# Reads of a compressive memory: full-array matmuls in the slot of the weighted sums, or matmuls on halves of the array's rows one slot later

## The chip, the cores and the metric

The kernel runs on one core of a Trainium2 chip. Five engines work side by side, each through its own instructions in order: TensorE (PE, matmuls and transposes, with weight loads shown apart as PEld), VectorE (DVE), ScalarE (ACT), GpSimd (POOL) and SyncE (SP, which here only issues DMAs). Matmuls write to PSUM, which the kernel uses as eight banks of 128 x 512 fp32; DVE and ACT read it. The metric is the device time of one execution in microseconds (us), the median of several.

## The reference

Four layers follow each other on x of 2048 rows by 512: A, B, A, B. A is linear attention with a learned feature map, B is attention in four segments of 512 rows with a memory that runs over the segments. The change is in B:

```python
phi = lambda t: jnp.where(t > 0, t + 1.0, jnp.exp(t))
for s in range(N):                      # N = 4 segments, H = 32 heads, Dh = 16
    qs, ks, vs = q[:, :, s], k[:, :, s], v[:, :, s]
    logits = jnp.einsum("bhqd,bhkd->bhqk", qs, ks) * scale + mask
    p = _softmax(logits, axis=-1)
    a_dot = jnp.einsum("bhqk,bhkd->bhqd", p, vs)
    pq = phi(qs)
    num = jnp.einsum("bhld,bhde->bhle", pq, M)
    den = jnp.einsum("bhld,bhd->bhl", pq, z)[..., None] + 1e-6
    a_mem = num / den
    o = g * a_mem + (1.0 - g) * a_dot
    outs.append(o)
    pk = phi(ks)
    M = M + jnp.einsum("bhld,bhle->bhde", pk, vs)
    z = z + jnp.einsum("bhld->bhd", pk)
```

A "read" is num, den and a_mem: the features of the queries against the memory M and its sums z. The memory is empty in the first segment, so segments 1 to 3 read it.

## The kernel before, in words

**Tiling.** Heads are handled in four chunks of eight (c = 0 to 3). The query features of one segment and chunk lie with 128 partitions (8 heads x 16) by 512 rows. A memory chunk `kn` is 128 partitions by 8 x 17 columns (16 values and one sum for each head), block diagonal: partitions 0 to 63 belong to heads 0 to 3 and 64 to 127 to heads 4 to 7, and the rest is zero. A read's output `ot` has 128 rows by four row blocks by 8 heads x 16.

**Order.** The program is fully unrolled, and the order is written out by hand. The helper `held` puts all matmuls and transposes in one fixed order on PE; the class `Ordered` does the same for DVE, ACT, POOL and SP: each engine executes in the order in which the Python code emits. In the profile all matmuls bear L178, transposes L182, and all other instructions L156, so groups are told by tile names and shapes.

**Slots.** The loop of B (`steps`) runs over slots k. Each unit of work m (four heads of one segment; 8 units a segment, 32 in all) takes R = 5 slots, named m.0 to m.4 within a segment. Each slot emits, in this order:

1. `attend`: one tile of logits into `lg` (PE), its exp by ACT into P, the masked blocks by POOL;
2. `maxima`: one step of row maxima for a later unit: products (PE) into `mx` and `my`, or in slots m.2 and m.4 (`SPARE`) into two banks of `g`, and their reduction by DVE ("CUSTOM_DVE_ANT_0 ... mask");
3. jobs that were put off to this slot, such as the low part `ta` of a projection (ACT copies the high part, DVE subtracts), and the DMAs that stack parts;
4. in m.0 alone `weighted`: P times v (PE, "g<-P,v"), evicted by ACT into U;
5. the words of the table's cell for this slot, left to right.

The tables FIRST, GAPS (segments 1 and 2), LAST and FINAL (segment 3 of the first and the second loop) hold the cells. The words that matter here: `a0` to `a3` one step of the read of chunk 0 to 3 (a `+` means the next segment); `max` transposes finished maxima ("g<-ident,mxs"), `fin` transposes U ("g<-ident,U"), weighs it on DVE and adds it to `ot` on POOL; `t`, `m` the two steps of a memory write; `ln` a step of a norm, which transposes x and makes its high and low parts; `Q`, `V`, `O` with `/6` six steps of a pair of projections, values or outputs; `v` work of the next layer. A pair is two accumulations at once on the two halves of the array's rows (`mm3_pair`); it takes its two banks of `g` at its first step in m.1 and gives them back after m.4.

**PSUM.** Tag `g` has four banks (G = 4), `lg` two, `mx` and `my` one each. A tile of `g` that finds all four in use waits until readers have finished with one.

**Weighing.** `weigh` takes a PSUM tile: DVE adds 1e-6 to the sums (reads only), takes reciprocals ("r<-r") and multiplies ("ot<-g,r"); for `fin` the product goes to `wt`, which POOL adds.

**The reads before.** `reads` has two steps, one for each half of the row blocks: one bank of `g`, two matmuls of 128 rows by 136 columns in fp32 ("g<-mem,tb"; each shows as two passes in the profile), one `weigh`. They stand in slots m.0, most often both steps ahead of `max` and `fin`.

Of the kernel before, what the change touches and what calls it, by code (L numbers as in the profile page):

```python
# [18 lines left out]
P = 128  # L19
# [3 lines left out]
VW = DH + 1  # L23
# [8 lines left out]
G = 4  # L32
# [27 lines left out]
4.0 max fin        | 4.1 Q0+/6 load    | 4.2 Q0+/6         | 4.3 Q0+/6 | 4.4 Q0+/6  # L60
5.0 t2 fin m2 max  | 5.1 V+/6          | 5.2 V+/6 n        | 5.3 V+/6 n | 5.4 V+/6
6.0 t3 fin m3 max  | 6.1 Q1+/6         | 6.2 Q1+/6 n       | 6.3 Q1+/6 n | 6.4 Q1+/6
7.0 a0+ a0+ max fin | 7.1 V+/6         | 7.2 V+/6 n        | 7.3 V+/6 n | 7.4 V+/6
"""
GAPS = """
0.0 a1 a1 max fin  | 0.1 Q2/6 n        | 0.2 Q2/6 n        | 0.3 Q2/6 n | 0.4 Q2/6
1.0 t0 turn fin m0 max | 1.1 Q3/6      | 1.2 Q3/6 n        | 1.3 Q3/6 | 1.4 Q3/6
2.0 turn t1 fin ln m1 max | 2.1 O/6    | 2.2 O/6           | 2.3 O/6 | 2.4 O/6
3.0 turn turn fin ln max | 3.1 O/6     | 3.2 O/6           | 3.3 O/6 | 3.4 O/6
4.0 ln ln a2 fin a2 max | 4.1 Q0+/6 load | 4.2 Q0+/6       | 4.3 Q0+/6 | 4.4 Q0+/6  # L70
5.0 t2 a3 fin m2 max | 5.1 V+/6 begin  | 5.2 V+/6 n N      | 5.3 V+/6 n N | 5.4 V+/6
6.0 a3 t3 fin m3 max | 6.1 Q1+/6       | 6.2 Q1+/6 n N     | 6.3 Q1+/6 n N | 6.4 Q1+/6
7.0 a0+ a0+ max fin | 7.1 V+/6         | 7.2 V+/6 n N      | 7.3 V+/6 n N | 7.4 V+/6
"""
LAST = """
0.0 a1 a1 max fin  | 0.1 Q2/6 n        | 0.2 Q2/6 n        | 0.3 Q2/6 n | 0.4 Q2/6
1.0 turn max fin   | 1.1 Q3/6          | 1.2 Q3/6 n        | 1.3 Q3/6 | 1.4 Q3/6
2.0 turn ln fin max | 2.1 O/6          | 2.2 O/6           | 2.3 O/6 | 2.4 O/6
3.0 turn turn fin ln max | 3.1 O/6     | 3.2 O/6           | 3.3 O/6 | 3.4 O/6
4.0 ln ln a2 fin a2 max | 4.1 v/2      | 4.2 v/2           | 4.3 v/2 | 4.4 v/2  # L80
5.0 a3 a3 max fin  | 5.1 v/1           | 5.2 v/1           | 5.3 v/1 | 5.4 v/1
6.0 max fin        | 6.1 v/1           | 6.2 v/1           | 6.3 v/1 | 6.4 v/1 pre
7.0 pt pt fin max  | 7.1 P/4           | 7.2 P/5           | 7.3 P/5 v/2 | 7.4 P/4 v/2
"""
FINAL = """
0.0 a1 a1 max fin  | 0.1 Q2/6          | 0.2 Q2/6          | 0.3 Q2/6 | 0.4 Q2/6
1.0 turn turn max fin | 1.1 Q3/6       | 1.2 Q3/6          | 1.3 Q3/6 | 1.4 Q3/6
2.0 max fin        | 2.1 O/6           | 2.2 O/6           | 2.3 O/6 | 2.4 O/6
3.0 a2 a2 max fin  | 3.1 O/6           | 3.2 O/6           | 3.3 O/6 | 3.4 O/6
4.0 turn turn fin max | 4.1 O/6        | 4.2 O/6           | 4.3 O/6 | 4.4 O/6  # L90
5.0 a3 a3 max fin  | 5.1 O/6           | 5.2 O/6           | 5.3 O/6 | 5.4 O/6
6.0 max fin pre    | 6.1 pt pt         | 6.2 P/6           | 6.3 P/6 | 6.4 P/6
7.0 pt pt max fin  | 7.1 P/4           | 7.2 P/5           | 7.3 P/5 | 7.4 P/4
"""
# [6 lines left out]
def interleave_kernel(ctx, tc, x_in, a_wqkv, a_wphi, a_wo, b_wq, b_wk, b_wv, b_wo, b_beta,  # L101
# [15 lines left out]
    def nm(s):  # L117
        uid[0] += 1
        return f"{s}_{uid[0]}"

    def T2(tag, bufs, dt=F32, shape=(P, 512)):
        return sp.tile(list(shape), dt, tag=tag, bufs=bufs, name=nm(tag))

    def PS(tag, bufs, shape=(P, 512)):
        return ps.tile(list(shape), F32, tag=tag, bufs=bufs, name=nm(tag))
# [40 lines left out]
    def held(i):  # L166

        if last[0] is not None:
            behind(i, last[0])
        last[0] = i  # L170
        return i
# [3 lines left out]
    def mm(*a, **k):  # L175
        n = a[0].free_size()
        work[0] += n / 2.26 if k["rhs"].dtype == F32R else (n * 2 / 2.4 + 25 if "tile_position" in k else 2 * max(112, n * 2 / 2.4))
        return held(nc.tensor.matmul(*a, **k))  # L178
# [339 lines left out]
    def weigh(out, p, eps, add, eng=pool):  # L518

        n, G = out.shape[1], out.shape[2]  # L520
        r = T2("r", 4, shape=(P, n, G))
        den = p[:, :, :, DH]
        if eps:
            dve.tensor_scalar(r, den, eps, None, op0=ADD)
            den = r
        dve.reciprocal(r, den)
        rb = r.unsqueeze(3).broadcast_to([P, n, G, DH])
        if not add:
            dve.tensor_tensor(out=out, in0=p[:, :, :, 0:DH], in1=rb, op=MUL)
            return  # L530
        t = T2("wt", 1, shape=(P, n, G, DH))
        dve.tensor_tensor(out=t, in0=p[:, :, :, 0:DH], in1=rb, op=MUL)
        eng.tensor_tensor(out=out, in0=out, in1=t, op=ADD)
# [441 lines left out]
    class LayerB:  # L975
# [96 lines left out]
        def reads(self, s, c):  # L1072

            kn = self.mem[:, c, 1]
            ph = self.st[s, c]["phi", 0]
            ot = self.sums(s, c).rearrange("p q (h d) -> p q h d", d=DH)
            for a in range(2):
                pn = PS("g", G)
                for q in range(2):
                    mm(pn[:, q * 8 * VW : (q + 1) * 8 * VW],  # L1080
                       lhsT=ph[:, (2 * a + q) * P : (2 * a + q + 1) * P], rhs=kn,
                       start=True, stop=True)
                weigh(ot[:, 2 * a : 2 * a + 2], pn[:, 0 : 16 * VW].rearrange("p (q h e) -> p q h e", q=2, h=8),
                      1e-6, False)
                yield

        def writes(self, s, c):

# [369 lines left out]
    for i in range(2):  # L1458
# [3 lines left out]
        a2 = la[i].pass2()  # L1462
# [40 lines left out]
```

## Time and profile before

| | |
|---|---|
| median of 3 runs | 1444.89 us (1442.71 to 1445.47) |
| the profiled execution | 1442.99 us |
| its span, first to last instruction | 1441.3 us |
| TensorE clock granted, mean | 0.997 |
| exps of the loops: 320 of 128 x 1024 on ACT | 329.3 us busy |
| reads on PE: 192 passes of 128 x 136 | 30.1 us busy |

How to read the lines: a group or a timeline row names the line, engine and operation, the tiles as out<-in, the shape (a matmul's shape is rows*columns of the array and then the moving operand), and xN for the number of instructions that were merged. In a timeline the first two columns are start and length in us; "[0.57 <-DVE mxs L156]" is idle time of the engine just before, and what ended it. A matmul's length includes its way through the pipeline, so the cost of one in a row of many is the distance of starts. A stretch lists, after its bounds and length, each engine's busy time in us with the number of instructions, then the granted clock, the DMA share and GB/s.

### The profile page before, as it was taken

What the parts mean: (1) busy time and instruction counts of PE and PEld (TensorE: products, weight loads), DVE (VectorE), ACT (ScalarE), POOL (GpSimd) and SP (SyncE); (2) the same over time, 40 slices, a digit from 0 to 9 for tenths busy, and PEclk for the clock granted to TensorE, in tenths of its full rate; (3) what the DMA queues carried; (4) which work ended last, traced back from release to release, by engine and by line L of the source; (5) the groups of instructions that cost most, each with busy time, mean ns of one, the idle gap of its engine ahead of it and who ended that gap; (6) DMA issues with size and microseconds to landing.
All of it is one profiled execution on the core that took longest, in us unless ns stands there. A gap on an engine that the chain in (4) does not pass through costs nothing.

```text
span 1441.3 us, 33697 instructions
## 1 busy us (share of the span) xinstructions
PE 1372.0 (95%) x12544; PEld 1049.0 (73%) x12544; DVE 1057.3 (73%) x3258; ACT 808.9 (56%) x1198; POOL 691.5 (48%) x1028
## 2 busy tenths in 40 slices
PE   7999989999999999999999999999999999999997
PEld 6887877776676776777568887887666767777764
DVE  4666778667787887888646767867768878878882
ACT  5545345436576577576634434453656756756653
POOL 1568665315447457335314446542335555654441
PEclk9999999999999999999999999999999999999998
DMA  5387356545444444445430103754453453443431
GB/s 193 115 317 270 127 159 192 161 118 154 119 126 141 117 132 137 118 130 166 141 125 22 60 30 129 249 171 120 125 178 97 131 157 97 130 130 97 112 91 59
DMA packets 108787, 196.06 MB, mean 136 GB/s; under 512 B 14416, under 2 KB 27856, under 8 KB 107856
## 3 DMA queue, kind: packets, MB, share of 16 engines
q1 hardware_dynamic: 107472, 193.38, 44.8%
q8 instruction: 100, 1.64, 0.5%
q10 hardware_dynamic: 1152, 0.52, 0.1%
q14 instruction: 63, 0.52, 0.1%
HBM read 101.05 MB, written 39.85 MB: 98 GB/s over the span
## 4 chain that ended last, share of the span: by engine, by line
PE 69%; DVE 12%; ACT 7%; POOL 5%; issue 3%; DMA 2%; SPq 1%; ACTq 0%; DVEq 0%; POOLq 0%
PE g L178 52%; PE lg L178 6%; PE g L182 5%; PE mx L178 3%; ACT P L156 3%; DVE es L156 2%; POOL tb L156 2%; POOL P L156 2%; PE lg L182 1%; PE my L178 1%; DVE g L156 1%; ACT U L156 1%; DMA wqk<-wqk 1%; DVE my L156 1%; DVE mx L156 1%
## 5 line engine op out<-in xcount | busy, mean ns | idle before, releaser
L156 ACT ACTIVATE P<-lg 128x1024 f32<-128x1024 f32 x320 | 329.3, 1029 | 176.9 <-PE lg L178 95.7
L156 POOL TENSOR_SCALAR_AFFINE_SELECT P<-P 128x256 f32<-128x256 f32 (+1 forms) x448 | 192.5, 444 | 327.3 <-ACT P L156 327.0
L156 DVE CUSTOM_DVE_ANT_0 mx<-mx,mask 128x128 f32<-128x128 f32 (+3 forms) x332 | 165.0, 497 | 42.6 <-PE my L178 37.8
L178 PE MATMUL g<-hh,wqk 64*128 64x512 f32 (+1 forms) x960 | 188.1, 392 | 3.5 <-DMA wqk<-wqk 2.0
L156 DVE CUSTOM_DVE_ANT_0 g<-g,mask 128x512 f32<-128x512 f32 x360 | 175.9, 543 | 15.2 <-PE g L178 14.4
L178 PE MATMUL g<-w,oh 64*128 64x512 f32 (+2 forms) x816 | 172.2, 385 | 6.8 <-SPq L156 5.0
L156 DVE CUSTOM_DVE_ANT_0 my<-my,mask 128x128 f32<-128x128 f32 (+3 forms) x332 | 172.0, 518 | 0.0
L178 PE MATMUL lg<-e,e 64*128 64x256 f32 (+2 forms) x1024 | 154.5, 353 | 14.5 <-ACT P L156 14.3
L178 PE MATMUL g<-P,v 128*32 128x512 f32 (+3 forms) x2048 | 151.1, 435 | 4.3 <-DVE mxs L156 4.0
L178 PE MATMUL g<-w,hh 64*128 64x512 f32 (+2 forms) x800 | 145.3, 357 | 0.6 <-DVE ol L156 0.6
L156 DVE DVE_READ_ACCUMULATOR2_ANT mxs<- 128x1 f32 x1024 | 143.2, 140 | 0.0
L178 PEld LDWEIGHTS lg<-e,e 64*128 64x128 f32 x1024 | 92.6, 185 | 64.3 <-ACT P L156 40.7
L178 PEld LDWEIGHTS g<-P,v 128*32 128x32 f32 x2048 | 59.7, 109 | 89.0 <-issue 63.8
L156 POOL TENSOR_SCALAR tb<-tb 128x512 f32<-128x512 f32 x72 | 110.9, 1552 | 25.4 <-ACT tb L156 22.1
L178 PEld LDWEIGHTS g<-hh,wqk 64*128 64x128 f32 (+1 forms) x960 | 108.2, 185 | 20.0 <-ACT hh L156 1.8
L178 PEld LDWEIGHTS g<-w,oh 64*128 64x128 f32 (+1 forms) x816 | 98.2, 188 | 28.9 <-SPq L156 9.6
L178 PE MATMUL g<-hl,wqk 64*128 64x512 f32 (+1 forms) x480 | 108.9, 390 | 0.5 <-DVE hl L156 0.5
L178 PE MATMUL g<-w,ol 64*128 64x512 f32 (+2 forms) x408 | 106.8, 379 | 1.0 <-DVE ol L156 1.0
L156 ACT COPY tb<-g 128x512 f32<-128x512 f32 (+1 forms) x148 | 80.9, 576 | 45.5 <-PE g L178 43.6
L178 PEld LDWEIGHTS g<-w,hh 64*128 64x128 f32 (+1 forms) x800 | 91.9, 187 | 13.3 <-DVE ol L156 1.0
L178 PE MATMUL g<-w,hl 64*128 64x512 f32 (+2 forms) x400 | 93.7, 355 | 0.0
L178 PE MATMUL mx<-e,e 63*128 63x256 f32 (+2 forms) x332 | 89.4, 331 | 0.3 <-DVE mxs L156 0.2
(148 smaller groups left out, 2917.3 us busy)
## 6 DMA issues: line engine op xcount, KB each, us to landing
e<-ta SPq DMA_DIRECT2D x384, 128.0 KB
wqk<-wqk SPq DMA_DIRECT2D x64, 512.0 KB
x<-x SPq DMA_DIRECT2D x48, 256.0 KB
ot<-in SPq DMA_DIRECT2D x28, 256.0 KB
pq<-tb SPq DMA_DIRECT2D x24, 256.0 KB
tb<-pq SPq DMA_DIRECT2D x24, 256.0 KB
x<-xr SPq DMA_DIRECT2D x22, 256.0 KB
xr<-x SPq DMA_DIRECT2D x20, 256.0 KB
```

Source lines behind the costliest of these rows:

```text
L156: i = f(*a, **k)
L178: return held(nc.tensor.matmul(*a, **k))
L182: return held(nc.tensor.transpose(*a))
```

## The change

The two steps of `reads` become one. It takes two banks of `g`, one for heads 0 to 3 and one for heads 4 to 7 of the chunk. For each of the four row blocks it issues two matmuls, on array rows 0 to 63 and 64 to 127, with 68 columns of `kn` each: the diagonal blocks alone. Then both banks are weighed. In the tables the word moves from m.0 to m.1, ahead of the pair in that cell; the two halves of a3, which stood in 5.0 and 6.0 in GAPS, come together in 5.1.

```diff
-7.0 a0+ a0+ max fin | 7.1 V+/6         | 7.2 V+/6 n        | 7.3 V+/6 n | 7.4 V+/6
+7.0 max fin        | 7.1 a0+ V+/6         | 7.2 V+/6 n        | 7.3 V+/6 n | 7.4 V+/6
...
 GAPS = """
-0.0 a1 a1 max fin  | 0.1 Q2/6 n        | 0.2 Q2/6 n        | 0.3 Q2/6 n | 0.4 Q2/6
+0.0 max fin        | 0.1 a1 Q2/6 n        | 0.2 Q2/6 n        | 0.3 Q2/6 n | 0.4 Q2/6
-4.0 ln ln a2 fin a2 max | 4.1 Q0+/6 load | 4.2 Q0+/6       | 4.3 Q0+/6 | 4.4 Q0+/6
-5.0 t2 a3 fin m2 max | 5.1 V+/6 begin  | 5.2 V+/6 n N      | 5.3 V+/6 n N | 5.4 V+/6
-6.0 a3 t3 fin m3 max | 6.1 Q1+/6       | 6.2 Q1+/6 n N     | 6.3 Q1+/6 n N | 6.4 Q1+/6
-7.0 a0+ a0+ max fin | 7.1 V+/6         | 7.2 V+/6 n N      | 7.3 V+/6 n N | 7.4 V+/6
+4.0 ln ln fin max       | 4.1 a2 Q0+/6 load | 4.2 Q0+/6       | 4.3 Q0+/6 | 4.4 Q0+/6
+5.0 t2 fin m2 max    | 5.1 a3 V+/6 begin  | 5.2 V+/6 n N      | 5.3 V+/6 n N | 5.4 V+/6
+6.0 t3 fin m3 max | 6.1 Q1+/6       | 6.2 Q1+/6 n N     | 6.3 Q1+/6 n N | 6.4 Q1+/6
+7.0 max fin         | 7.1 a0+ V+/6         | 7.2 V+/6 n N      | 7.3 V+/6 n N | 7.4 V+/6
...
 LAST = """
-0.0 a1 a1 max fin  | 0.1 Q2/6 n        | 0.2 Q2/6 n        | 0.3 Q2/6 n | 0.4 Q2/6
+0.0 max fin        | 0.1 a1 Q2/6 n        | 0.2 Q2/6 n        | 0.3 Q2/6 n | 0.4 Q2/6
-4.0 ln ln a2 fin a2 max | 4.1 v/2      | 4.2 v/2           | 4.3 v/2 | 4.4 v/2
-5.0 a3 a3 max fin  | 5.1 v/1           | 5.2 v/1           | 5.3 v/1 | 5.4 v/1
+4.0 ln ln fin max       | 4.1 a2 v/2      | 4.2 v/2           | 4.3 v/2 | 4.4 v/2
+5.0 max fin        | 5.1 a3 v/1           | 5.2 v/1           | 5.3 v/1 | 5.4 v/1
...
 FINAL = """
-0.0 a1 a1 max fin  | 0.1 Q2/6          | 0.2 Q2/6          | 0.3 Q2/6 | 0.4 Q2/6
+0.0 max fin        | 0.1 a1 Q2/6          | 0.2 Q2/6          | 0.3 Q2/6 | 0.4 Q2/6
-3.0 a2 a2 max fin  | 3.1 O/6           | 3.2 O/6           | 3.3 O/6 | 3.4 O/6
+3.0 max fin        | 3.1 a2 O/6           | 3.2 O/6           | 3.3 O/6 | 3.4 O/6
-5.0 a3 a3 max fin  | 5.1 O/6           | 5.2 O/6           | 5.3 O/6 | 5.4 O/6
+5.0 max fin        | 5.1 a3 O/6           | 5.2 O/6           | 5.3 O/6 | 5.4 O/6
...
-            for a in range(2):
-                pn = PS("g", G)
-                for q in range(2):
-                    mm(pn[:, q * 8 * VW : (q + 1) * 8 * VW],
-                       lhsT=ph[:, (2 * a + q) * P : (2 * a + q + 1) * P], rhs=kn,
-                       start=True, stop=True)
-                weigh(ot[:, 2 * a : 2 * a + 2], pn[:, 0 : 16 * VW].rearrange("p (q h e) -> p q h e", q=2, h=8),
-                      1e-6, False)
-                yield
+            pns = [PS("g", G)[:, 0 : 16 * VW] for _ in range(2)]
+            for q in range(4):
+                for a, pn in enumerate(pns):
+                    mm(pn[:, q * 4 * VW : (q + 1) * 4 * VW], lhsT=ph[64 * a : 64 * a + 64, q * P : (q + 1) * P],
+                       rhs=kn[64 * a : 64 * a + 64, 4 * a * VW : (4 * a + 4) * VW], start=True, stop=True,
+                       tile_position=(64 * a, 0))
+            for a, pn in enumerate(pns):
+                weigh(ot[:, :, 4 * a : 4 * a + 4], pn.rearrange("p (q h e) -> p q h e", q=4, h=4), 1e-6, False)
+            yield

```

## The prediction

> **What bounds the kernel now.** I read the page's busy shares first, then the by-engine line of the chain of waits, and then the stretch of the first attention loop.
>
> ```profile
> PE 1372.0 (95%) x12544; PEld 1049.0 (73%) x12544; DVE 1057.3 (73%) x3258; ACT 808.9 (56%) x1198; POOL 691.5 (48%) x1028
> ...
> PE 69%; DVE 12%; ACT 7%; POOL 5%; issue 3%; DMA 2%; SPq 1%; ACTq 0%; DVEq 0%; POOLq 0%
> ...
> 310.00:740.00 430.00, 412.19 (x4065) 300.38 (x4062) 325.97 (x1220) 277.45 (x399) 202.71 (x349) 1.00 0.47 134
> ```
>
> PE sets the end; in the loop it is busy 412 of 430 us. DVE is third in busy time (326 us of 430), but it matters here because PE hands it PSUM banks. The clock was granted in full, so no clock effect enters. Next, the tile view of the memory state gives the reads, and the timeline shows one of them, a1 in slot 0.0, and the two slots behind it (columns: start, length, engine, line, operation).
>
> ```profile
> L178 PE MATMUL g<-mem,tb x192: 279/279/384, 399.2 to 1393.6; 128*128 128x136 f32 x192
> ...
> 519.79 1.19 PE L178 MATMUL g<-mem,tb 128*128 128x136 f32 x8
> 519.92 0.69 ACT L156 ACTIVATE U<-g,share 128x512 f32<-128x512 f32 x1 [0.79 <-PE g L178]
> 520.56 0.17 DVE L156 TENSOR_SCALAR r<-g 128x16 f32<-128x16 f32 x1 [0.98 <-PE g L178]
> 520.82 0.27 PE L182 MATMUL g<-ident,mxs 128*16 128x128 f32 x1
> 520.93 0.60 PE L182 MATMUL g<-ident,U 128*128 128x128 f32 x4
> 521.05 0.42 DVE L156 TENSOR_TENSOR ot<-g,r 128x256 f32<-128x256 f32 x1
> 521.39 0.16 DVE L156 TENSOR_SCALAR r<-g 128x16 f32<-128x16 f32 x1
> 521.46 0.50 PE L178 MATMUL lg<-e,e 64*128 64x512 f32 x2
> 521.79 0.28 PE L178 MATMUL mx<-e,e 63*128 63x256 f32 x1
> 522.22 0.25 DVE L156 RECIPROCAL r<-g 128x16 f32<-128x16 f32 x1
> 522.50 0.42 DVE L156 TENSOR_TENSOR wt<-g,r 128x256 f32<-128x256 f32 x1
> 522.84 0.29 DVE L156 CUSTOM_DVE_ANT_0 mx<-mx,mask 128x128 f32<-128x128 f32 x1
> 523.49 0.46 PE L178 MATMUL lg<-e,e 64*128 64x256 f32 x4
> 523.78 0.39 PE L178 MATMUL g<-e,e 63*128 63x512 f32 x2
> 524.33 0.73 DVE L156 CUSTOM_DVE_ANT_0 g<-g,mask 128x512 f32<-128x512 f32 x1
> ```
>
> There are 192 read passes: 24 reads of four matmuls, each in two passes. Eight of them take 520.82 - 519.79 = 1.03 us with some 0.10 us for the first weights, so 0.93 us, or 0.116 us each. PE then transposes the maxima and U, and slot 0.1 begins with lg at 521.46. Nothing on PE waits. On DVE one weighing takes 0.83 us to the next (520.56 to 521.39) and 0.91 us to its own end (521.05 + 0.42), finish's weighing 0.62 (522.22 to 522.84), and the four maxima of slot 0.1 take 1.49 (522.84 to 524.33). The maxima of slot 0.2 start on PE at 523.78, which is 2.32 us behind the lg of 0.1.
>
> **The reads themselves: no time saved.** After, each read is 8 matmuls of 64 rows by 68 columns, 16 passes, in 8 pairs if the two halves run together. The trace has no fp32 row halves, so I bound a pair by its nearest rows: column halves with 68 columns below, row halves with the same 128 weight columns above.
>
> ```profile
> L178 PE MATMUL g<-KN,P 128*64 128x68 f32 x1024 | 38.2, 226 | 6.6 <-ACT P L156 6.6
> ...
> 201.85 1.17 PE L178 MATMUL g<-KN,P 128*64 128x68 f32 x32 [0.72 <-ACT P L156]
> ...
> 401.55 0.40 PE L178 MATMUL g<-w,hh 64*128 64x256 f32 x4
> 401.79 0.28 PE L178 MATMUL g<-w,hl 64*128 64x256 f32 x2
> ```
>
> The first: 16 pairs in 1.17 us less the last one's 0.23 of its own, 0.059 us each. The second: two pairs from 401.55 to 401.79, 0.12 us each. The shorter one loads 64 weight columns, the other 128 as the reads do, so I take 0.118: a read costs 8 x 0.118 = 0.94 us instead of 0.93. Bounds: 0.47 us, and 16 x 0.116 = 1.86 us if the halves do not overlap at all. The first read pass bears on this: it lasts 384 ns instead of 279, 105 ns longer for weights that nothing hides. The weighing's new view, four blocks of four heads, costs nothing: finish's product has that view already, and both products take 0.42 us (521.05, 522.50).
>
> The Trainium skill (TensorE: Matmul & The Clock Gate, section LDWEIGHTS) says that a weight load's time follows its columns and not its rows, about 107 ns for 128; the trace's 105 ns agrees. By it the halved rows do not make the loads shorter, and a read would cost 8 x 0.107 = 0.86 us, near my value.
>
> **The place: what the reads covered in x.0.** They stood between the weighted sums and the transposes, while ACT evicted U. Slots that have no read show what happens without them.
>
> ```profile
> 704.52 0.69 ACT L156 ACTIVATE U<-g,share 128x512 f32<-128x512 f32 x1 [1.47 <-PE g L178]
> 705.26 0.66 PE L182 MATMUL g<-ident,U 128*128 128x128 f32 x4 [0.60 <-ACT U L156]
> 705.95 0.26 DVE L156 RECIPROCAL r<-g 128x16 f32<-128x16 f32 x1 [1.74 <-PE g L182]
> ```
>
> U's transposes start 0.05 us after U's end (705.21) and wait 0.60 us; DVE starts 0.03 us after their end. So with the a1 read gone they start at 519.92 + 0.69 + 0.05 = 520.66 instead of 520.93: slot 0.0 gets 0.27 us shorter and not 0.93. The lg of 0.1 starts 0.53 us after that, at 521.19.
>
> **The two banks: a new wait in x.2.** Tag g has four banks. In x.1 the read now takes two and the pair of projections or outputs behind it takes the other two and keeps them to x.4. In x.2 the maxima ask for two g banks: only the read's can be free, and these come free when DVE has weighed both. DVE works in program order, so ahead of that stand finish's weighing, the four maxima of x.1 and, in some slots, the subtraction that makes a low part. For a1: U transposed at 520.66 + 0.60 = 521.26, DVE starts 521.29, finish 0.62 to 521.91, maxima 1.49 to 523.40 (their scores come at 521.52 + 0.28), weighings 0.83 + 0.91 to 525.14, bank seen by PE 0.05 later, 525.19. Before it was 523.78: **+1.41 us**. PE by itself would be there at 521.19 + 2.03 + 0.94 + 0.29 = 524.45, so 0.74 of this is waiting. Queued behind the waiting maxima on PE are that slot's six pairs, the next lg, and with it ACT's next exp. The halves' price hardly enters: a shorter read only lengthens the wait, and the 1.86 bound ends 0.5 us after DVE is free here.
>
> The same sum for the other reads, each with the rows it needs:
>
> ```profile
> 507.63 0.69 ACT L156 ACTIVATE U<-g,share 128x512 f32<-128x512 f32 x1 [0.86 <-PE g L178]
> 511.50 0.39 PE L178 MATMUL g<-e,e 63*128 63x512 f32 x2
> 512.11 0.69 DVE L156 TENSOR_TENSOR ta<-tb,ta 128x512 fp32r<-128x512 f32 x1
> 512.72 0.69 DVE L156 CUSTOM_DVE_ANT_0 g<-g,mask 128x512 f32<-128x512 f32 x1
> ...
> 576.57 0.16 DVE L156 TENSOR_SCALAR r<-g 128x16 f32<-128x16 f32 x1
> 579.42 0.40 PE L178 MATMUL g<-e,e 63*128 63x512 f32 x2
> ...
> 591.14 0.30 DVE L156 CUSTOM_DVE_ANT_0 mx<-mx,mask 128x128 f32<-128x128 f32 x1 [0.45 <-PE my L178]
> 592.80 0.40 PE L178 MATMUL g<-e,e 63*128 63x512 f32 x2
> ...
> 1392.86 0.69 ACT L156 ACTIVATE U<-g,share 128x512 f32<-128x512 f32 x1 [1.47 <-PE g L178]
> 1396.47 0.40 PE L178 MATMUL g<-e,e 63*128 63x512 f32 x2
> ...
> 399.37 0.69 ACT L156 ACTIVATE U<-g,share 128x512 f32<-128x512 f32 x1 [0.87 <-PE g L178]
> 402.60 0.56 PE L178 MATMUL lg<-e,e 64*128 64x256 f32 x4 [0.18 <-ACT P L156]
> 403.00 0.40 PE L178 MATMUL g<-e,e 63*128 63x512 f32 x2
> 409.17 2.36 PE L178 MATMUL g<-P,v 128*32 128x512 f32 x32 [0.57 <-DVE mxs L156]
> ```
>
> - a0+, full slots (4 reads): as a1, with the subtraction ahead (512.11 to 512.72, 0.61): U's end 508.32 + 0.05 + 0.60 + 0.03 + 0.62 + 1.49 + 0.61 + 1.74 + 0.05 = 513.51, before 511.50: +2.01.
> - a2 in 4.1 (5 reads): DVE is free of the low parts of the columns at 576.57 whatever the reads do: + 0.62 + 1.49 + 1.74 + 0.05 = 580.47, before 579.42: +1.05.
> - a3 of the first two read segments (4 reads): before, half stands in 5.0 and half in 6.0. In 5.0 the writes' transposes cover U, so the first maximum moves from 591.14 to 591.06 at best: + 1.49 + 0.61 + 1.74 + 0.05 = 594.95, before 592.80: +2.15, less the half read taken out of 6.0, 4 x 0.116 = 0.47: +1.68.
> - a3 of the first loop's last segment, a2 and a3 of the second's (3 reads; the pairs behind them are half as wide or half as many): 1393.55 + 0.05 + 0.60 + 0.03 + 0.62 + 1.49 + 1.74 + 0.05 = 1398.13, before 1396.47: +1.66. In these slots PE waits some 0.2 us for exp (402.60); two such waits go: +1.26.
> - The first a0+ of each loop (2 reads): 400.06 + 5.19 = 405.25, before 403.00: +2.25, less 0.4 of such waits, less the 0.57 that PE waits for DVE at 409.17: +1.28.
>
> **Sum**: 6 x 1.41 + 4 x 2.01 + 5 x 1.05 + 4 x 1.68 + 3 x 1.26 + 2 x 1.28 = 8.5 + 8.0 + 5.3 + 6.7 + 3.8 + 2.6 = 34.8 us. The profiled execution took 1442.99 us (span 1441.3 and 1.7 around it), a little under the median of 1444.89. 1442.99 + 34.8 = 1477.8: **1478 us**. DVE's instructions, PE's transposes, ACT, POOL and the DMAs stay in number and order otherwise, and nothing is moved past a DMA.
>
> **Rivals.**
> 1. The halves do not overlap: 1.86 us a read. For speaks that two passes of one half follow each other; against, that the P,v and KN,P groups overlap their column parts. Where DVE is free at lg + 2.21 (a1 and the three of the last segments), PE's result comes 0.5 us later: 9 x 0.5 = 4.5, so 1482.
> 2. The bank wait does not bind, since the maxima get other banks or DVE is ahead of my order; U's lost cover stays. Then 15 reads cost 0.94 - 0.27 = 0.67 each, a2 nothing, a3 0.94 - 0.08 - 0.47 = 0.39: 10.0 + 1.6 = 11.6, so 1455. Against it speak the four banks and DVE's order, which the code fixes.
> 3. Not slower: the halves run at the short pair's 0.059, 0.47 us a read, and the banks do not bind. Then 11.6 - 24 x 0.46 = 0.6, so 1443; it decides from the point where a read's two weighings end before PE reaches x.2's maxima, and each further 0.1 us that a read saves is then 2.4 us. The 0.059 row speaks for it, the 0.12 row and the 105 ns against it.
>
> Rival 3 is also what the Trainium skill (TensorEngine Tiling (Array Packing), Theoretical Speedup) would give for a contraction of 64, up to twice as fast; its PSUM Bottleneck section warns that eviction does not get faster, which is my forecast's mechanism. The trace so far shows the first for column halves alone.
>
> **How the numbers follow.** Forecast 0.65, with its own range 1466 to 1487 (exp waits and the DVE pitches off by a quarter); rival 1 0.12; rival 2 0.14; rival 3 0.09. A measurement here can tell some 0.2%, 2.9 us, from no change. Rival 3 splits into faster 0.05, same 0.03 and slower 0.01; all else is slower: 0.92. The range 1450 to 1488 leaves out rival 3 and a tail on each side.
>
> **What would show it.** Right: in x.2 the g maxima wait for DVE's ot some 0.7 us behind a1 and 1.3 behind a0+; U's transposes wait for ACT U in 7.0 and 0.0; the x.1 maxima on DVE start earlier than before, the x.2 ones later; a pair of read passes starts each 0.11 to 0.12 us. Wrong: no idle time of PE before x.2's maxima, pairs at 0.06, or PE's total idle time (69 us now) not up by 20 us or more.

## The result and the profile after

The changed kernel takes 1487.72 us (median of 4 runs, 1485.99 to 1490.09) where the kernel before, beside it, takes 1445.01: 42.7 us more, a ratio of 1.0303 with a 95% interval of 1.0285 to 1.0322. The forecast was 34.8 us more and 1478 us; the direction and the mechanism hold, the size is 8 us short, and the time lies just under the top of the range given, 1488 us, while the ratio's interval (1486.2 to 1491.5 us on 1445.01) reaches past it. One of the four executions of e3 below took 3346.14 us, the other three 1472.38 to 1475.10; its ratio leaves that one out.

The page of the changed kernel, and the stretch of the first loop (the loop runs past 740 us now, so the stretch cuts it earlier than before):

```profile
PE 1387.6 (93%) x12736; PEld 1063.9 (72%) x12736; DVE 1063.1 (72%) x3258; ACT 805.9 (54%) x1198; POOL 690.9 (47%) x1028
...
PE 64%; DVE 15%; ACT 8%; POOL 5%; issue 4%; DMA 3%; SPq 1%; ACTq 0%; POOLq 0%; DVEq 0%
...
310.00:740.00 430.00, 401.37 (x4016) 297.66 (x4016) 322.11 (x1205) 266.93 (x387) 199.38 (x343) 1.00 0.46 129
```

The granted clock is the same, 0.997; PE is busy 401 of 430 us instead of 412, its idle time over the whole span rose from 69 to 97 us, and in the chain of waits DVE has 15% instead of 12%. What PE waited for, first in the kernel before (total us, times, longest):

```profile
PE g L182 <- ACT U L156: 5.6, 14, 0.8
...
PE g L178 <- DVE mxs L156: 4.0, 9, 0.8
```

and then in the changed one:

```profile
PE g L182 <- ACT U L156: 14.9, 37, 0.8
PE g L178 <- DVE r L156: 12.8, 18, 1.3
...
PE g L178 <- DVE ot L156: 5.8, 16, 0.4
...
PE g L178 <- DVE tmp L156: 2.9, 8, 0.4
PE g L178 <- DVE mxs L156: 2.3, 4, 0.8
```

Both forecast waits are there. U's transposes wait for ACT 37 times instead of 14, and three rows are new: PE waits 42 times for the weighings ("r", and the read's outputs "ot" and "tmp"). The a1 read that the prediction followed looks like this now, first the tile view of the reads (x192 counts a sample of the 384) and then the timeline. "PEld" is the load of weights into the array:

```profile
L178 PE MATMUL g<-mem,tb x384: 219/272/273, 403.7 to 1438.8; 64*128 64x68 f32 x192
...
531.25 0.28 PE L182 MATMUL g<-ident,mxs 128*16 128x128 f32 x1
531.39 0.69 ACT L156 ACTIVATE U<-g,share 128x512 f32<-128x512 f32 x1 [0.91 <-PE g L178]
532.13 0.42 PEld L182 LDWEIGHTS g<-ident,U 128*128 128x128 f32 x4 [0.79 <-ACT U L156]
532.13 0.66 PE L182 MATMUL g<-ident,U 128*128 128x128 f32 x4 [0.60 <-ACT U L156]
532.72 0.50 PE L178 MATMUL lg<-e,e 64*128 64x512 f32 x2
532.83 0.26 DVE L156 RECIPROCAL r<-g 128x16 f32<-128x16 f32 x1 [1.93 <-PE g L182]
533.06 0.28 PE L178 MATMUL mx<-e,e 63*128 63x256 f32 x1
533.18 0.33 PE L178 MATMUL mx<-e,e 63*128 63x384 f32 x1
533.36 1.01 PE L178 MATMUL g<-mem,tb 64*128 64x68 f32 x16
533.55 0.30 DVE L156 CUSTOM_DVE_ANT_0 mx<-mx,mask 128x128 f32<-128x128 f32 x1
534.17 0.47 PE L178 MATMUL g<-hh,wqk 64*128 64x512 f32 x2
535.05 0.17 DVE L156 TENSOR_SCALAR r<-g 128x16 f32<-128x16 f32 x1
535.54 0.42 DVE L156 TENSOR_TENSOR ot<-g,r 128x256 f32<-128x256 f32 x1
535.62 0.46 PE L178 MATMUL lg<-e,e 64*128 64x256 f32 x4
535.88 0.16 DVE L156 TENSOR_SCALAR r<-g 128x16 f32<-128x16 f32 x1
536.11 0.46 PE L178 MATMUL g<-e,e 63*128 63x512 f32 x1
536.37 0.43 DVE L156 TENSOR_TENSOR ot<-g,r 128x256 f32<-128x256 f32 x1
536.72 0.70 DVE L156 CUSTOM_DVE_ANT_0 g<-g,mask 128x512 f32<-128x512 f32 x1
536.94 0.47 PE L178 MATMUL g<-e,e 63*128 63x512 f32 x1 [0.37 <-DVE ot L156]
```

DVE idles 1.93 us until U is transposed, then finishes (532.83), takes the four maxima (533.55), and comes to the read only at 535.05. PE could start the products for the maxima of m.2 behind lg (535.62 + 0.29 = 535.91, with 0.29 as before the change, 523.49 to 523.78). The first bank is free after the first product (535.54 + 0.42), and the matmul for it starts at 536.11; the second bank's waits to 536.94. The recorded idle time, 0.37 us, is only part of this: the matmul at 536.11 counts as busy while its twin waits. So the three new rows (21.5 us) understate the wait.

For the whole sum I took the distances of starts on PE: for each of the 24 reads the time from the first P,v matmul of its unit's m.0 to the lg of m.1, from lg to lg through m.4, and to the next P,v, in the changed kernel less the kernel before (us, sums over 24 reads; the experiments are read in the same way below).

```
                              m.0     m.1     m.2   m.3+m.4  to P,v     sum
the changed kernel          -10.1   +20.1   +31.2    +2.7    -0.1   +43.9
e1 place alone              -10.0   +29.2   +22.7    +2.3    +0.1   +44.2
e2 halves alone              +3.3    -0.1     0.0     0.0    +2.9    +6.1
e3 other banks               -7.4   +20.2    -1.3    +0.4   +19.6   +31.4
e4 changed, no addition     -10.1   +20.3   +21.4    +1.9    -0.1   +33.5
e5 before, no addition       -0.4     0.0     0.0    +0.3    -0.9    -1.0
e6 split                     -6.5   +18.1   +14.0    +2.2    -0.2   +27.7
e7 no reads                 -10.1    +0.9    -0.5    +2.1    -1.1    -8.6
e8 read first               -8.4    +20.7    -0.5    +1.2   +11.6   +24.6
e9 read first, no addition  -10.1   +20.1    -1.3    +0.3    +7.7   +16.7
```

The intervals between these units give 1.6 us back in the changed kernel (the half of a3 that left 6.0 gives back 2.1, and the others scatter). Its profiled execution also reaches the logits of the first loop 2.3 us later, 1.3 us of it in the wait for the first DMA, which the change doesn't touch.

### The profile page after: what moved, and what is told of

Same layout as the page of the kernel before. It is cut to its first block, busy times and chain, and to the rows that moved or that the text cites. A ratio compares the mean times of both kernels' runs of the same rounds, so it can differ in the third digit from the quotient of the medians.

```text
span 1485.1 us, 34078 instructions
## 1 busy us (share of the span) xinstructions
PE 1387.6 (93%) x12736; PEld 1063.9 (72%) x12736; DVE 1063.1 (72%) x3258; ACT 805.9 (54%) x1198; POOL 690.9 (47%) x1028
## 4 chain that ended last, share of the span: by engine, by line
PE 64%; DVE 15%; ACT 8%; POOL 5%; issue 4%; DMA 3%; SPq 1%; ACTq 0%; POOLq 0%; DVEq 0%
PE g L178 48%; PE lg L178 6%; PE g L182 5%; ACT P L156 3%; PE mx L178 3%; ACT U L156 2%; DVE es L156 2%; POOL tb L156 2%; POOL P L156 2%; DVE r L156 2%; DVE my L156 2%; DVE mx L156 1%; PE my L178 1%; DMA wqk<-wqk 1%; PE lg L182 1%
## 5 line engine op out<-in xcount | busy, mean ns | idle before, releaser
L178 PE MATMUL g<-hh,wqk 64*128 64x512 f32 (+1 forms) x960 | 200.7, 395 | 3.7 <-DMA wqk<-wqk 2.3
L178 PE MATMUL g<-w,oh 64*128 64x512 f32 (+2 forms) x816 | 172.7, 385 | 6.6 <-SPq L156 4.8
L178 PE MATMUL lg<-e,e 64*128 64x256 f32 (+2 forms) x1024 | 164.7, 351 | 12.4 <-ACT P L156 12.1
L178 PE MATMUL g<-w,hh 64*128 64x512 f32 (+2 forms) x800 | 156.6, 363 | 0.6 <-DVE ol L156 0.6
L178 PE MATMUL g<-P,v 128*32 128x512 f32 (+3 forms) x2048 | 151.1, 435 | 2.6 <-DVE mxs L156 2.3
L178 PEld LDWEIGHTS lg<-e,e 64*128 64x128 f32 x1024 | 104.4, 185 | 54.4 <-ACT P L156 33.6
L178 PEld LDWEIGHTS g<-hh,wqk 64*128 64x128 f32 (+1 forms) x960 | 121.8, 185 | 19.1 <-issue 2.5
L178 PEld LDWEIGHTS g<-P,v 128*32 128x32 f32 x2048 | 58.7, 109 | 87.9 <-issue 65.0
L178 PE MATMUL g<-hl,wqk 64*128 64x512 f32 (+1 forms) x480 | 119.9, 391 | 0.5 <-DVE hl L156 0.5
L178 PEld LDWEIGHTS g<-w,oh 64*128 64x128 f32 (+1 forms) x816 | 98.8, 187 | 28.3 <-SPq L156 9.4
L178 PE MATMUL g<-e,e 63*128 63x256 f32 (+2 forms) x456 | 91.2, 343 | 21.6 <-DVE r L156 12.8
L178 PEld LDWEIGHTS g<-w,hh 64*128 64x128 f32 (+1 forms) x800 | 102.0, 188 | 11.2 <-DVE ol L156 1.0
L178 PE MATMUL g<-w,ol 64*128 64x512 f32 (+2 forms) x408 | 108.0, 380 | 1.0 <-DVE ol L156 1.0
L178 PE MATMUL g<-w,hl 64*128 64x512 f32 (+2 forms) x400 | 104.9, 357 | 0.0
```

## The experiments

The theory: DVE's weighings hold the two banks that the maxima of m.2 need, U has lost its cover, and the halves are neutral. Rival A: the halves themselves cost. Rival B: the bank wait is no cause, since DVE's lateness would come due anyway. Rival C: the reads cost their whole PE time wherever they stand. The diffs show parts; "..." marks what is left out.

**e1, place alone**: full-array reads, both steps in m.1.

```diff
-7.0 a0+ a0+ max fin | 7.1 V+/6
+7.0 max fin        | 7.1 a0+ a0+ V+/6
...
```

> Place alone: the reads stay full-array matmuls in two steps (one bank each), but both steps stand in m.1 ahead of the pair. Theory (bank wait in m.2 for DVE's weighings, plus U's lost cover; the halves are neutral): like the changed kernel, 1480 to 1495 us, with the wait before the maxima of m.2 still there (0.7 to 1.3 us a read). Rival A (the row halves themselves cost, by their weight loads or because the two halves fall out of step): near before, 1445 to 1455.

Measured: 1488.04 us, ratio 1.0309 (1.0290 to 1.0328). Rival A falls: the place alone is the whole loss. The waits of e1:

```profile
PE g L182 <- ACT U L156: 14.9, 37, 0.8
...
PE g L178 <- DVE r L156: 7.2, 18, 0.9
...
PE g L178 <- DVE ot L156: 4.8, 16, 0.4
```

The table tells more: in m.1 the full-array reads need 9.1 us more than the halves (29.2 to 20.1), and in m.2 they wait 8.5 us less. So the halves do save PE time in m.1, 0.38 us a read, and nearly all of it turns into waiting. In the a1 read followed above the matmul for the second bank starts 7.97 us after P,v in e1 and 7.98 in the changed kernel: DVE sets when m.2 goes on.

**e2, halves alone**: the new `reads`, one word in m.0 where the last two stood.

```diff
-0.0 a1 a1 max fin  | 0.1 Q2/6 n
+0.0 a1 max fin  | 0.1 Q2/6 n
...
```

> Halves alone: the new reads on row halves into two banks, in m.0 where the full-array steps stood (a3 in 5.0). Theory: 1443 to 1450 us; 8 pairs x 0.112 = 0.89 us for 0.93 saves 1 us over 24 reads, one more change between whole and halved array each time may cost some 2. Rival A: most of the loss stays, 1465 or more.

Measured: 1446.71 us, 1.0018 (1.0006 to 1.0029), as forecast. In m.0 the halves save nothing; the whole of a3 in 5.0 costs 0.67 us a read there, for the half that leaves 6.0. The 2.9 us at the next P,v, 0.36 us behind each a0+ for the most part, were not followed up.

**e3, other banks**: in units with a read, the maxima use `g` in m.3 alone.

```diff
-                if self.k >= 0 and self.k % R in SPARE:
+                if self.k >= 0 and self.k % R in ((3,) if self.k // R in self.read_units else SPARE):
...
```

> The changed kernel, but in units with a read the maxima of m.2 and m.4 use mx and my and those of m.3 use g, so the maxima of m.2 need no bank that the read holds. Theory: the idle time before those maxima (DVE r 12.8 + DVE ot 5.8 + DVE tmp 2.9 = 21.5 us in the changed kernel) goes, most of it from the time: 1464 to 1472 us. Rival B (only U's lost cover and the read's own PE time cost; the bank wait is time that DVE would make PE lose later in any case): 1480 or more, with the idle time moved to other slots.

Measured: 1474.51 us, 1.0206 (1.0183 to 1.0228): 13 us less than the changed kernel, not the 16 to 24 expected. The rows that waited for the weighings are gone but for 0.3 us, and e3 has a new one:

```profile
PE mx L178 <- DVE mxs L156: 9.3, 15, 1.4
```

In the table m.2's 31.2 us are gone, and 19.6 come back in the next unit's m.0, where PE now waits for the maxima of m.4. Rival B is partly right.

**e4 and e5, less DVE work**: no addition of 1e-6 in the reads, in the changed kernel and in the one before.

```diff
-                weigh(ot[:, :, 4 * a : 4 * a + 4], pn.rearrange("p (q h e) -> p q h e", q=4, h=4), 1e-6, False)
+                weigh(ot[:, :, 4 * a : 4 * a + 4], pn.rearrange("p (q h e) -> p q h e", q=4, h=4), 0.0, False)
```

> The changed kernel without the addition of 1e-6 to the sums of the reads (two DVE instructions a read less, 0.20 us each to the next; the term 1e-6 of the denominator is left out). Theory: DVE's order ahead of the bank sets the wait in all 24 reads, so 24 x 0.41 = 9.8 us less: 1476 to 1481. Rivals A and B: no more than 2 us less, 1485 to 1488.

> The kernel before without the addition of 1e-6 in the reads (left out of the denominator; 9.8 us of DVE time in all). Theory: before the change nothing waited for the weighings, so 1442 to 1446, against -9.2 in the changed kernel. Rival B (DVE's work is on the path wherever it stands): 1437 or less.

Measured: e4 1478.52 us, 1.0241 (1.0219 to 1.0262), 9.2 us less than the changed kernel for the 9.8 us of DVE time, and m.2 lost 9.8 of its 31.2. e5 0.9994 (0.9979 to 1.0009): the same DVE instructions cost nothing where the reads stood before. The two together show that DVE's weighings set the pace of these slots after the change and did not before it.

**e6, split**: full-array steps, one in m.0 and one in m.1.

```diff
-7.0 a0+ a0+ max fin | 7.1 V+/6
+7.0 a0+ max fin | 7.1 a0+ V+/6
...
```

> Full-array reads, one step in m.0 as before and one in m.1. Theory: half a read in m.0 still covers most of U, so m.0 loses some 0.3 us a read, m.1 gains 0.47, and the maxima of m.2 wait for one weighing instead of two (0.83 us less): 0.8 (a1) to 1.4 us (a0+) a read, 20 to 30 us: 1465 to 1475. Rival A or a price that goes with the number of reads moved: half of the change, 1466, with the waits of m.2 at half.

Measured: 1472.07 us, 1.0185 (1.0168 to 1.0202), within the expectation; m.2 grew by 14.0 us instead of 31.2, near half, so the sum does not tell the two explanations apart. The kinds of reads do: against the changed kernel m.2 grows by 0.10 us instead of 0.90 in a1, by 0.27 instead of 1.07 in the last a3 and a2, and by 0.70 instead of 1.50 in a0+. That is 0.80 us less each time, about one weighing (0.83), as the theory says, and not half; a3 and the first a0+ lose 0.78 and 0.80 too. Only a2 differs (0.92 instead of 1.35, with 0.71 us less given back in m.0). And with one step left in m.0, the U wait is back at 6.4 us.

**e7, no reads**: the kernel before with no read.

```diff
-                  pt.rearrange("p (q h e) -> p q h e", q=4, h=4), 0.0, s > 0,
+                  pt.rearrange("p (q h e) -> p q h e", q=4, h=4), 0.0, False,
...
                 elif op == "a":
-                    next(reads[s, i])
+                    pass
```

It leaves out the memory's part of the output, and `finish` writes `ot` where it added to it.

> The kernel before without any read (the memory's part of the output is left out, and finish writes ot instead of adding to it). Theory: most of the reads' 22 us on PE lay in the time that the transposes have to wait for ACT's U anyway, so the time falls by what m.0 gained in the changed kernel, 10 us, and 2 more from m.6: 1428 to 1435. Rival C (the reads cost their whole PE time where they stood): 1422 or less.

Measured: 1430.87 us, 0.9902 (0.9880 to 0.9924), 14.5 us less. The 192 passes take 192 x 0.116 = 22.3 us on PE, so at least a third of that was free: it lay in the time that U's transposes have to wait for ACT. (The distances between the loops' P,v give 12.2 us: 8.6 in the table and 3.6 outside it.) DVE and POOL lose the reads' work as well; e5 shows no gain from a part of DVE's. Rival C falls. The same -10.1 us in m.0 as in the changed kernel says that moving the reads away gave back only this.

**e8, the read first**: in m.1 the read is emitted before the maxima and the put-off jobs, so DVE weighs first.

```diff
+            READ = ("a0+", "a1", "a2", "a3")
...
+                put_off[0] = None
+                for w in table.get(k, ((), 0))[0]:
+                    if w in READ:
+                        do(w, table[k][1], k)
                 if -LEAD <= k < R * N - LEAD:
                     next(ma)
...
-                    do(w, s, k)
+                    if w not in READ:
+                        do(w, s, k)
```

> The changed kernel, but the read of a cell is emitted before the maxima and the put-off jobs of its slot m.1, so that on DVE its two weighings stand ahead of the four maxima and the subtraction (1.5 to 2.1 us). The reads stay in m.1, on row halves, in two banks. Theory: the banks are free when PE comes to the maxima of m.2, that slot loses its +31 us, and what stays is m.0's -10 and m.1's +20: 1452 to 1460 us. Rival B (DVE's lateness comes due somewhere else, as the bank change above moved 19.6 us into the next unit's m.0): 1470 or more.

Measured: 1470.72 us, 1.0172 (1.0150 to 1.0193): 17 us less than the changed kernel, but 11 above the expectation. The wait in m.2 is gone but for 1.4 us in four places, and a part returns elsewhere:

```profile
PE g L178 <- DVE mxs L156: 10.8, 16, 1.3
```

Here P times v of the next m.0 waits for banks whose maxima DVE has not yet taken; +11.6 us in the table. The theory had to be widened: it is not only the order on DVE, but where DVE has time. This is what DVE's weighings waited for in the kernel before (the read's by g L178, finish's by g L182):

```profile
DVE r L156 <- PE g L182: 34.2, 15, 4.9
...
DVE r L156 <- PE g L178: 25.3, 25, 2.0
```

in the changed one:

```profile
DVE r L156 <- PE g L182: 75.9, 38, 4.9
...
DVE r L156 <- PE g L178: 2.1, 2, 1.0
```

and in e8:

```profile
DVE r L156 <- PE g L182: 73.7, 36, 4.9
...
DVE r L156 <- PE g L178: 14.2, 21, 1.1
```

DVE idles in m.0 in any case, until PE has something for it, and the two rows together grew from 59.5 to 78.0 us with the change. (In m.0 of the 24 units alone, DVE's gaps over 0.06 us grew from 33.7 to 47.6 us.) Before, the weighings began in that time. Now some 1.7 us of them a read come later, into m.1 to m.4. In the changed kernel DVE has idle time there, 14.1 us in m.3 alone, because PE is late from its wait in m.2. In e8 it has none at all in m.2 to m.4 of the 24 units, so what is late is made up for only in the next m.0. But e8 also makes a wait of its own: the weighings now stand ahead of the maxima, and DVE idles 14.9 us in m.1 (5.4 in the changed kernel) until the read's matmuls are done. How the 11.6 us divide between the two was not measured.

**e9, the read first, and no addition.** It tests the widened theory.

> The kernel with the read ahead of m.1's maxima, and without the addition of 1e-6 (left out of the denominator). Theory as it now stands: DVE's work moved from m.0, where it idles, into m.1 to m.4, where it is busy throughout; the 11.6 us that came back in the next unit's m.0 stand behind 13 of the 24 reads (a0+, a3 and the last a2), so 13 x 0.41 = 5.3 us less: 1463 to 1467. If the returning wait is not DVE's amount of work but its order: 1469 or more.

Measured: 1462.52 us, 1.0124 (1.0096 to 1.0152), just below the expected span. The returning wait falls from 11.6 to 7.7 us in the table; by the medians the step from e8 is 0.48%, 6.9 us, with intervals that touch. The rival, 1469 or more, falls. By kind the returning wait fits in part: behind the eight a3 and full-slot a0+ it falls by 0.41 us each, the DVE time of the two additions; behind the two first a0+ it stays at 1.07 us, and behind the three last reads it hardly moves (0.43 to 0.41).

**e10, spread**: the kernel before, with the steps of the last segments moved under U waits that had no cover.

```diff
-4.0 ln ln a2 fin a2 max | 4.1 v/2
-5.0 a3 a3 max fin  | 5.1 v/1
-6.0 max fin        | 6.1 v/1
+4.0 ln ln a2 fin max | 4.1 v/2
+5.0 a2 a3 max fin  | 5.1 v/1
+6.0 a3 max fin     | 6.1 v/1
...
```

> The kernel before, with the reads left in m.0 as they are, but in the last segment of each loop their steps are spread so that a slot which waits for U without any cover gets one: LAST a2 in 4.0 and 5.0, a3 in 5.0 and 6.0; FINAL a2 in 2.0 and 3.0, a3 in 5.0 and 6.0. Theory: a step under the U wait is free (0.46 of 0.60 us), a step out of 4.0 saves 0.65, a step out of a slot with two saves 0.27: 0.65 + 2 x 0.27 = 1.2 us less, 1443 to 1445 beside 1445. Rivals: no change at all, or slower by the steps' full 0.47 each.

Measured: 1442.71 us (median of 12 executions) beside 1442.98, 0.9989 (0.9975 to 1.0003). The sign and the size agree with the 1.2 us expected, but the interval holds no change, so a gain isn't shown. No version that computes the whole reference beats the kernel before by more than can be measured.

## What the prediction had right, and the step that failed

- **The reads save nothing on halves: the reason was right, a part of the price not.** Pairs of passes start 0.11 us apart, near the 0.118 taken and far from the lower bound of 0.059; eight take 0.81 us with the first weights loaded ahead (533.36 to 534.17), where the prediction took 0.94. The longer m.1, 0.88 to 0.90 us in full slots, is a little under that 0.94. That full-array reads would cost 0.38 us more in m.1 (e1) was not in the prediction; it is nearly without effect, as the prediction said of the halves' price. Why they cost 1.32 us in a1's m.1 and 0.93 in m.0 is open.
- **U's cover: right.** m.0 gives back 10.1 us: 0.27 us in each a1, as worked out there; 0.21 in a0+ and the last reads, where 0.27 was taken; nothing in a3, where 0.08 was; and 1.31 in each a2, for which the prediction wrote down no term (its second rival lets a2 come out at nothing, so 0.94). U's transposes start 0.05 us after U, as taken.
- **The bank wait: right in mechanism, place and order, and mis-sized.** This is the step that failed: its chain from U's transposes to the second bank, and with it the term for m.3, m.4 and the next m.0, which it put at nothing except behind the first a0+. PE's wait for the second bank is 1.0 us behind a1 and 1.6 behind a0+, where some 0.7 and 1.3 were forecast.
- **The chain, link by link, for a1 from 532.13.** The transposes take 0.66 us instead of 0.60: the weights of the first are loaded only when U is there (the PEld row at 532.13), and the second starts 0.165 us behind it, the others 0.109 apart. The row at 705.26, quoted in the prediction, had said 0.66 already. The first maximum comes 0.72 us after the start of finish instead of 0.62. The prediction took its scores as ready at lg + 0.33 + 0.28, the end of the first of two products into `mx`; the second ends later (533.18 + 0.33 = 533.51), and the maximum starts at 533.55. In eight a1 and a0+ reads this distance is 0.04 us each time, where before the change it was about 0.6, so by these distances it now waits for PE's scores and not for DVE's own work. PE starts on a bank 0.15 us after DVE's last product, not the 0.05 that holds behind ACT. With 0.03 of rounding the second bank is 0.28 us later than forecast.
- **What that is worth in time.** Up to the lg of m.3 the 24 units lose 41.2 us, where the prediction's terms give 8.5 + 8.0 + 5.3 + 8.6 + 3.8 + 3.7 = 37.8 (a3 before 6.0, the first a0+ before the 0.57): 3.4 us from the chain. (In the a1 followed here 0.10 of the 0.28 us is made up by that lg; one of the two products has run by then.) From m.3 to the next P,v 2.7 us are lost, where the terms gave 1.1 back: 3.7 to 3.8 us. The half that left 6.0 gives back 2.1 instead of 1.9. Why m.3 and m.4 grow is open.
- **By kind** (predicted, measured from the distances, a3 with what 6.0 gives back): a1 1.41, 1.71; a0+ 2.01, 2.34; a2 1.05, 1.26; a3 1.68, 1.92; the last a3 and a2 1.26, 1.49; the first a0+ 1.28, 1.86. Summed with their counts 34.8 and 41.8. The first a0+ is off most. Its two waits for ACT's exps, at the lg of m.2 and of m.3, do go and the 0.57 us at the next P,v comes back, as forecast, but m.3 and m.4 grow, by 0.93 us in the first loop and 0.10 in the second. So its mean rests on one large value, whose cause is open.
- **The rivals of the prediction.** Halves that do not overlap: wrong, they pair. A bank wait that does not bind: wrong, m.2 grew by 31 us. Not slower: wrong on both of its conditions.
- **What the prediction did not see** is why the wait cannot be mended by order or banks alone: e3 and e8 take it out of m.2, and 19.6 and 11.6 us return in the next m.0. The prediction argued with DVE's order; DVE's free time was in m.0.

## What to carry to other kernels

Before moving work out of a stretch, look at what it hides there for other engines (here ACT's eviction, so that 22 us of matmuls were worth 14.5) and at what its followers on other engines do with their time: a move on PE moved 1.7 us of DVE work a read out of a stretch where DVE waits into one where, with the bank wait mended in e8, it had no time left. When pricing a chain that starts with a new stall, take the lengths from rows that follow a stall, and ask at each link for all that the instruction needs: what was ready long before can now come last. And where two banks are asked for together, the recorded idle time understates the wait: compare starts.

## What the hardware showed beyond this

PE took up a bank that DVE had released 0.15 us after the end of DVE's instruction (536.37 + 0.43 to 536.94 in rounded rows; 0.146 to 0.147 for both banks of all 24 reads of the changed kernel), and U 0.05 us after ACT's (531.39 + 0.69 to 532.13; the same in the 19 reads that wait for it). Pairs of fp32 passes on row halves with 128 weight columns start every 0.11 us though only 68 columns stream, nearly as far apart as full-array passes of 136 columns, 0.116.
